# Attention fused with a four-expert layer: loads reordered and one group's start moved, values a head later, block sums spread over the steps, a broadcast put ahead of the transposes

## Chip, cores, metric

One core of one Trainium2 chip. The metric is the device time of one execution in microseconds (us). "Span" is the length of the one execution that was profiled; it is about 1.7 us shorter than its time.

## The reference, cut to what matters

```python
# attention: 4 batches x 8 heads x 768 positions x 64, causal
#   heads 0, 2, 6 ("retrieval"): full causal mask
#   heads 1, 3, 4, 5, 7 ("streaming"): 4 sink keys + a window of 64
a = exp(scale * q @ k.T, masked);  a = a / a.sum();  x = a @ v        # -> x: 3072 x 512
# mixture: 4 experts, every token goes through all of them
out = sum_e p[:, e] * (relu(x @ w1[e]) @ w2[e])                        # w1: 512 x 1024, w2: 1024 x 512
```

## The kernel before

The program puts every engine's instructions into a fixed order. Attention is done in 8 groups of 384 rows (group g = batch g // 2, half g % 2); its steps are laid between the experts' matmuls by a plan. The first 3 row tiles go through the experts plainly, then one tile alone ("the one-tile phase"), then 10 pairs of tiles. In a pair the second layer is done with seven products of block sums instead of eight products of blocks, and the inputs are scaled by the probabilities beforehand (`scale_inputs`, writing `xs`).

Names in code and profile: kRr and kSr are key rows as loaded, for the retrieval and the streaming heads; from group 2 on SyncE's DMA transposes make kR and kS of them, and qT of the queries q. vR and vS are values, es the exponentials of the scores. xT holds the attention's result, scaled and transposed, as the experts' input; pB is the broadcast of the probabilities. pA, pV and pO are PSUM tiles, the buffers that TensorE writes to. hA holds an expert's inner results and, in the first phases, finished rows. Line numbers differ between kernels: L1049, L1052, L1058 and L1059 are the same matmul, the pairs' first layer.

```python
# attention of one group (g > 0): a head's values come one head behind its scores
for n, h in enumerate(order):
    v_steps, done = iter(()), None
    if waiting:
        done = waiting.pop(0)
        v_steps = values(done)
    yield from both(scores(h), v_steps)
    ...
    waiting.append(h)
if more:                                   # the next group's transposes, on SyncE
    if g == 1:
        transpose_rows(*more)              # 3 x qT <- q, then kR <- kRr (retrieval keys)
    transpose_windows(*more)               # sinks <- kSr, kSr <- sinks (a patch), kS <- kSr
for h in waiting:
    yield from values(h)

# pair: expert by expert
for e in range(E):
    if e + 1 < E:
        scale_inputs(nt0, e + 1)           # VectorE, 1.2 us: xs of the next expert
    ...                                    # 4 steps: 8 matmuls, then relu on ScalarE
    if e == 1:
        input_sums(0, 2 * HT)              # VectorE, three sums at once
    elif e > 1:
        input_sums(e * HT, (e + 1) * HT)
# then seven products; values() and PSUM:
ps = pV.tile([P, 512], FP32, name="pV", bufs=2)    # two buffers for all heads' values

def loads(a):                              # GpSimd; called for a = 2 to 7
    b, c = divmod(a, NCH)
    load_k(b, c, RH)                       # kRr: 3 loads
    load_k(b, c, SH)                       # kSr: 5 loads, wait until the last kS has landed
    load_q(b, c)                           # 3 loads
    if b == 1:
        one_values_r(gp, b, c)
    load_v(b, c, RH)                       # vR: 3 loads

# (UNIT, ONE, PAIR: the TensorE time of an expert of the first phase, of the one-tile phase, of a pair)
begin = E * UNIT
for a, n in zip(range(2, G), (0.6, 1.65, 3.2, 4.65, 6.2, 7.65)):
    plan[a] = (begin, first_pair + n * PAIR)
    begin = plan[a][1]
```

The softmax here doesn't subtract the row's maximum and nothing guards it: scores larger than these inputs give would overflow.

## Time and profile before

| | before |
|---|---|
| time, median of runs (first measurement) | 409.35 us |
| span of the profiled run | 407.7 us |
| TensorE busy | 380.9 us (93%) |
| TensorE idle | 26.8 us, of which kR 7.9, scaled inputs 6.7 |

How to read it: TensorE is the engine that everything serves, so time is lost only where it stands still or where its granted clock is low. The list of its waits says for what it stood still (total, how often, longest); the matmuls in order of time, each with its wait in brackets, say where; a table of stretches gives the clock. The lines are in the prediction.

### The profile page before, as it was taken

How to read it: one execution, taken by the hardware profiler on the slowest of the kernel's cores; microseconds unless marked ns; L12 is line 12 of the kernel's file. 1: busy time of each engine (PE TensorE's matmuls, PEld its weight loads, DVE VectorE, ACT ScalarE, POOL GpSimd, SP SyncE). 2: the span in 40 equal slices, each digit the busy share in tenths (PEclk: the TensorE clock that was granted, in tenths of full speed). 3: DMA queues.
4: the chain of work that ended last, by engine and by line, in shares of the span. 5: the costliest groups of instructions: out<-in, count | busy, mean ns of one | idle time of the engine just before them, and what ended most of it. 6: DMA issues, size and time to landing. Idle time of an engine off the chain costs nothing.

```text
span 407.7 us, 9337 instructions
## 1 busy us (share of the span) xinstructions
PE 380.9 (93%) x3814; PEld 314.4 (77%) x3814; DVE 220.5 (54%) x472; ACT 231.1 (57%) x476; POOL 138.9 (34%) x182
## 2 busy tenths in 40 slices
PE   7799999659799998999999999999999999999996
PEld 4654555347588887888988898889988898888885
DVE  7745876506466366556455367466455366344350
ACT  4654568226397479276584478366674486351631
POOL 8824744944524544282227215181200000000000
PEclk9999999969899999999999999999999999999999
DMA  8999999999989999999499939899670110110101
GB/s 158 166 207 198 189 160 149 129 126 233 146 85 183 83 119 159 156 148 172 54 178 113 115 45 156 181 121 148 83 158 25 57 57 7 51 54 2 53 0 53
DMA packets 167631, 47.67 MB, mean 117 GB/s; under 512 B 156492, under 2 KB 161316, under 8 KB 167588
## 3 DMA queue, kind: packets, MB, share of 16 engines
q0 software_dynamic: 102656, 20.98, 70.8%
q1 hardware_dynamic: 63332, 25.70, 29.3%
q8 instruction: 30, 0.49, 0.5%
q10 hardware_dynamic: 1600, 0.39, 0.5%
q14 instruction: 13, 0.11, 0.1%
HBM read 48.82 MB, written 6.34 MB: 135 GB/s over the span
## 4 chain that ended last, share of the span: by engine, by line
PE 48%; DVE 6%; ACT 5%; issue 1%; ACTq 0%
PE pO L1078 25%; PE pA L1049 19%; ACT hA L1058 3%; DVE hA L916 3%; PE pA L627 2%; DVE xs L1025 2%; DVE hA L1031 1%; ACT es L645 1%; PE pV L675 1%; PE pV L739 1%; ACT rc L757 1%; DVE es L649 0%; ACT rc L767 0%; ACT o L1137 0%; ACTq L1137 0%
## 5 line engine op out<-in xcount | busy, mean ns | idle before, releaser
L1049 PE MATMUL pA<-xs,w1sb 128*128 128x256 f16 x1280 | 154.9, 274 | 6.7 <-DVE xs L1025 6.7
L1049 PEld LDWEIGHTS <-w1sb 128*128 128x128 f16 x1280 | 121.6, 98 | 23.6 <-DVE xs L1025 9.2
L1058 ACT ACTIVATE hA<-pA 128x512 f16<-128x512 f32 x160 | 94.6, 598 | 42.5 <-PE pA L1049 38.3
L1078 PEld LDWEIGHTS <-hA 128*128 128x128 f16 x1120 | 107.1, 98 | 12.8
L645 ACT ACTIVATE es<-pA 128x384 f16<-128x384 f32 (+2 forms) x122 | 60.5, 510 | 44.2 <-PE pA L627 42.0
L1078 PE MATMUL pO<-w2sb,hA 128*128 128x256 f16 x640 | 76.3, 272 | 0.0
L1078 PE MATMUL pO<-tsb,hA 128*128 128x256 f16 x480 | 58.2, 273 | 0.0
L281 POOL DMA_DIRECT2D vS<-in_v_dram x30 | 29.4, 980 | 75.8 <-PE pV L739 75.6
L1025 DVE TENSOR_TENSOR xs<-xT,pB 128x1024 f16<-128x1024 f16 (+1 forms) x52 | 49.4, 972 | 8.3 <-PE pA L1049 8.2
L233 POOL DMA_DIRECT2D kSr<-in_k_dram x30 | 29.3, 985 | 51.7 <-DMA kS<-kSr 46.0
L916 DVE TENSOR_TENSOR hA<-hA 128x1024 f16<-128x1024 f16 (+1 forms) x80 | 41.8, 553 | 3.8 <-PE pO L1078 2.6
L947 PE MATMUL pA<-xT,w1sb 128*128 128x384 f16 (+1 forms) x256 | 33.6, 283 | 0.1
L627 PE MATMUL pA<-qT,kR 128*128 128x384 f16 (+2 forms) x120 | 24.9, 280 | 8.8 <-DMA kR<-kRr 7.9
L960 ACT ACTIVATE hA<-pA 128x384 f16<-128x384 f32 (+1 forms) x64 | 22.6, 386 | 17.6 <-PE pA L947 16.4
L649 DVE TENSOR_TENSOR es<-es,mC 128x256 f16<-128x256 f16 (+1 forms) x42 | 10.8, 258 | 39.3 <-ACT es L645 39.0
L968 PE MATMUL pO<-w2sb,hA 128*128 128x512 f16 x128 | 31.3, 381 | 0.6 <-DMA w2sb<-in_moe_w_dram 0.6
L649 DVE TENSOR_TENSOR es<-es,mS 128x384 f16<-128x384 f16 (+1 forms) x40 | 13.9, 348 | 30.6 <-ACT es L645 30.6
L1099 DVE TENSOR_TENSOR o<-pO,s 128x256 f32<-128x256 f32 x30 | 12.7, 424 | 31.2 <-PE pO L1078 30.1
L947 PEld LDWEIGHTS <-w1sb 128*128 128x128 f16 x256 | 21.1, 103 | 8.6 <-issue 0.7
L1031 DVE TENSOR_TENSOR hA<-hA 128x512 f16<-128x512 f16 (+1 forms) x30 | 15.3, 511 | 21.9 <-ACT hA L1058 21.5
L762 DVE TENSOR_TENSOR xT<-pV,rc 64x384 f16<-64x384 f32 x37 | 20.5, 554 | 11.4 <-ACT rc L767 9.1
L1096 ACT COPY s<-pO 128x256 f32<-128x256 f32 x30 | 11.2, 372 | 27.0 <-PE pO L1078 26.8
(113 smaller groups left out, 342.4 us busy)
## 6 DMA issues: line engine op xcount, KB each, us to landing
pB<-p_rows SPq DMA_DIRECT2D x10, 512.0 KB
out_dram<-o SPq DMA_DIRECT2D x19, 256.0 KB
w1sb<-in_moe_w_dram POOLq DMA_DIRECT2D x8, 512.0 KB, 9.9
w2sb<-in_moe_w_dram POOLq DMA_DIRECT2D x4, 1024.0 KB, 13.2
kSr<-in_k_dram POOLq DMA_DIRECT2D x30, 112.0 KB, 5.2
vS<-in_v_dram POOLq DMA_DIRECT2D x30, 112.0 KB, 4.3
q<-in_q_dram POOLq DMA_DIRECT2D x18, 128.0 KB, 5.7
vR<-in_v_dram POOLq DMA_DIRECT2D x24, 48.0 KB, 4.9
```

Of the source, the lines that this page charges most:

```text
L233: gp.dma_start(out=kSr[:, :, SH.index(h), own(h)], in_=windows_of(k, b, h, c),)
L281: gp.dma_start(out=t[:, :, own_v(h)], in_=windows_of(v, b, h, c))
L627: nc.tensor.matmul(out=ps[:, o : o + nq], lhsT=key_tile(b, c, h, t), rhs=qTs[b, c][:, hp, q0 : q0 + nq], start=(n == 0 or not first), stop ...
L645: nc.scalar.activation(out=es[:, 0:cols], in_=ps[:, 0:cols], func=AF.Exp, scale=SC)
L649: nc.vector.tensor_tensor(out=es[:, o0:o1], in0=es[:, o0:o1], in1=m[:, mo : mo + o1 - o0], op=ALU.mult,)
L916: nc.vector.tensor_tensor(out=out, in0=a, in1=b, op=ALU.subtract)
L947: nc.tensor.matmul(out=pss[ft][:, 0:cols_n], lhsT=w1sb[:, e * DMP + ct, ft * P : (ft + 1) * P], rhs=x[:, ct, :], start=(n == 0), stop=(n = ...
L968: nc.tensor.matmul(out=ps_o, lhsT=hs[:, ft, j * P : (j + 1) * P], rhs=w2sb[:, e * FTP + ft, :], start=(ft == 0), stop=(ft == FTP - 1),)
L1025: nc.vector.tensor_tensor(out=o, in0=xin, in1=pb.to_broadcast([P, DMP, n, P]), op=ALU.mult)
L1049: nc.tensor.matmul(out=ps[:, f * PC : (f + 1) * PC], lhsT=w1sb[:, e * DMP + ct, (f0 + f) * P : (f0 + f + 1) * P], rhs=xs[:, ct, :], start= ...
L1058: nc.scalar.activation(out=blocks[:, b0 : b0 + 2, k0 : k0 + 2, :].rearrange("p t f x -> p f t x"), in_=ps.rearrange("p (f t x) -> p f t x" ...
L1078: nc.tensor.matmul(out=ps, lhsT=a[:, k, :], rhs=b(k), start=(first and k == 0), stop=(k == KT - 1), skip_group_check=not first,)
```

## The change

Its intent is to fill the 7.9 us in which TensorE waits for the first transposed keys of group 2, and the small waits inside each pair. In words: group 2's attention starts 0.6 of the one-tile phase later; q and vR are loaded ahead of kSr (the diff does it for all groups from 2 on); the broadcast pB of the probabilities goes ahead of group 2's transposes on SyncE; block sums go one per step behind the scaled inputs; and values may stand two heads behind the scores.

```diff
@@ attention
-                if waiting:
+                ahead = sum(len(score_tiles(x)) for x in (*waiting, h))
+                if len(waiting) > 1 or (waiting and ahead > 6):
                     done = waiting.pop(0)
@@
                 if g == 1:
+                    load_probs(pair0)
                     transpose_rows(*more)
@@ pair_steps (input_sums now returns its three operations)
+                if sums:
+                    sums.pop(0)()
                 yield 2 * DMP * mm_ns(PC), 1.0
             if e == 1:
-                input_sums(0, 2 * HT)
+                sums += input_sums(0, 2 * HT)
             elif e > 1:
-                input_sums(e * HT, (e + 1) * HT)
+                sums += input_sums(e * HT, (e + 1) * HT)
+        for op in sums:
+            op()
@@ products (cut: the two S4 sums go from behind product 2 to behind products 3 and 4)
-        if nxt is not None:
-            scale_inputs(nxt, 0)           # behind product 3
...
+        if nxt is not None:
+            scale_inputs(nxt, 0)           # behind product 5
@@ moe_steps
-        load_probs(pairs[0])
@@ loads
         load_k(b, c, RH)
-        load_k(b, c, SH)
         load_q(b, c)
         ...
         load_v(b, c, RH)
+        load_k(b, c, SH)
@@ plan
-    begin = E * UNIT
-    for a, n in zip(range(2, G), (0.6, 1.65, ...)):
+    begin = E * UNIT + 0.6 * ONE
+    for a, n in zip(range(2, G), (0.66, 1.65, ...)):
```

More of the change, by code (lines that the diff above doesn't have):

```diff
@@ L876 @@
     p_rows = tc.dram_tile([NTILE, E * P], FP32, name="p_rows")
+    pair0 = 4
     def turn_probs():
@@ L1030, in input_sums, with s1 @@
         k = slice(k0, k1)
-        nc.vector.tensor_tensor(
-            out=S1[:, k, :], in0=A21[:, k, :], in1=A22[:, k, :], op=ALU.add
-        )
-        minus(S3[:, k, :], A11[:, k, :], A21[:, k, :])
-        minus(S2[:, k, :], S1[:, k, :], A11[:, k, :])
+        def s1():
+            nc.vector.tensor_tensor(
+                out=S1[:, k, :], in0=A21[:, k, :], in1=A22[:, k, :], op=ALU.add
+            )
+        return [
+            s1,
+            lambda: minus(S3[:, k, :], A11[:, k, :], A21[:, k, :]),
+            lambda: minus(S2[:, k, :], S1[:, k, :], A11[:, k, :]),
+        ]
     def pair_steps(nt0, nxt):
+        sums = []
         for e in range(E):
@@ L1106, in store, with fourth_sum @@
             nc.sync.dma_start(out=out[r, c], in_=o[:, i, c])
+        def fourth_sum(n):
+            k = slice(n * KT // 2, (n + 1) * KT // 2)
+            minus(S4[:, k, :], A12[:, k, :], S2[:, k, :])
         last = nxt is None
@@ L1113, in pair_steps @@
         yield from product(y, A12, b(1, 0), True)
-        for k in range(0, KT, KT // 2):
-            minus(S4[:, k : k + KT // 2, :], A12[:, k : k + KT // 2, :], S2[:, k : k + KT // 2, :])
-            if k == 0:
-                add(0, y, 0, 0)
+        add(0, y, 0, 0)
         yield half
@@ L1120, in pair_steps @@
         keep(1, x)
-        if nxt is not None:
-            scale_inputs(nxt, 0)
+        fourth_sum(0)
         yield half
@@ L1125, in pair_steps @@
         keep(2, y)
+        fourth_sum(1)
         yield half
@@ L1142, in pair_steps @@
         yield half
-    pair0 = 4
     pairs = list(range(pair0, NTILE, PT))
@@ L1192 @@
     plan = {1: (1.15 * UNIT, 3.5 * UNIT)}
-    begin = E * UNIT
-    for a, n in zip(range(2, G), (0.6, 1.65, 3.2, 4.65, 6.2, 7.65)):
+    begin = E * UNIT + 0.6 * ONE
+    for a, n in zip(range(2, G), (0.66, 1.65, 3.2, 4.65, 6.2, 7.65)):
         plan[a] = (begin, first_pair + n * PAIR)
```

## The prediction

> **What bounds the kernel now.** I read the page's parts 1 and 2, then TensorE's waits, then the matmuls of the disturbed stretch in order of time, then DVE's and the queues' order there. TensorE does nearly everything: 380.9 of 407.7 us.
>
> ```profile
> PE 380.9 (93%) x3814; PEld 314.4 (77%) x3814; DVE 220.5 (54%) x472; ACT 231.1 (57%) x476; POOL 138.9 (34%) x182
> ...
> PEclk9999999969899999999999999999999999999999
> ```
>
> So only 26.8 us of TensorE's span are idle, and the most that any reordering can win is that plus matmul time spent at a lower clock: the clock row dips in slices 9 and 11 (82 to 92 us and 102 to 112 us). The waits by cause:
>
> ```profile
> PE pA L627 <- DMA kR<-kRr: 7.9, 1, 7.9
> PE pA L1049 <- DVE xs L1025: 6.7, 8, 2.6
> PE pV L739 <- DVE es L649: 1.6, 4, 0.6
> PE pV L675 <- ACT es L645: 1.4, 4, 0.8
> ...
> PE pV L739 <- DVE xT L762: 1.1, 1, 1.1
> ```
>
> One wait for a key transpose and eight waits for scaled inputs are 14.6 us. The matmul timeline shows where:
>
> ```profile
> 78.10 0.39 PE L947 MATMUL pA<-xT,w1sb 128*128 128x128 f16 x4
> 86.38 0.61 PE L627 MATMUL pA<-qT,kR 128*128 128x128 f16 x2 [7.89 <-DMA kR<-kRr]
> ...
> 106.94 1.61 PE L1049 MATMUL pA<-xs,w1sb 128*128 128x256 f16 x8 [2.58 <-DVE xs L1025]
> ...
> 121.51 1.05 PE L1049 MATMUL pA<-xs,w1sb 128*128 128x256 f16 x8 [0.92 <-DVE xs L1025]
> ```
>
> The stretches behind the two long gaps run at about half clock:
>
> ```profile
> 86.20:90.20 4.00, 3.82 (x32) 3.38 (x33) 0.29 (x1) 2.35 (x8) 2.29 (x3) 0.50 0.59 68
> 106.90:110.40 3.50, 3.46 (x24) 2.62 (x25) 1.48 (x2) 0.98 (x2) 0.16 (x1) 0.55 2.47 182
> ```
>
> Columns: stretch, length, then busy time of PE, PEld, DVE, ACT, POOL, granted clock, DMA share, GB/s. Half clock costs 4.0 x 0.50 = 2.0 us behind the first gap and 3.5 x 0.45 = 1.6 us behind the second.
>
> **What the skill says.** "TensorE: Matmul & The Clock Gate", Part 1 (The HAM clock gate): idling for about one window of 3.4 us drops the array to half clock, and about 3.4 us of sustained work brings it back. The trace agrees on the way back (4.0 and 3.5 us at 0.50 to 0.55), while here 2.58 us of idling was enough; gaps of about 1 us cost no clock. "DMA: Bandwidth & Descriptors", Issuing engines are not separate DMA queues: transfers of SyncE and GpSimd interleave on the same 16 engines. So another load moved in front of a transpose delays it; how much, no row of the trace isolates. "Perfetto Trace Analysis", Optimization Strategy, advises interleaving regimes with different limits; that is what this change does with attention (bound there by loads) and the expert matmuls.
>
> **The change, part by part.** No engine gets more arithmetic: the order listing has the same instructions on all engines, only moved.
>
> 1. *Group 2's attention later.* Before, the first score of group 2 stands right after 4 of the 128-column matmuls (78.10). Now some 2.3 of the 4 experts of the one-tile phase stand in front of it. One expert there is 32 x 0.062 + 8 x 0.217 = 3.7 us (28 of L947 took 1.74 us at full clock, 4 of L968 took 0.87), so the first score is wanted 3.7 + 3.7 + 1.75 = 9.2 us after 77.5, at about 86.7.
>
> 2. *Group 2's loads in another order.* In GpSimd's timeline the three q loads are issued at 69.9 to 72.5, behind five kSr loads of which the last two waited for weights (64.15 and 68.94). With the order turned, q takes the slots at 59.8 to 62.9, and landed about 71 by my estimate (it still shares the queue with weights that land at 68.9). SyncE, which issued the qT transposes at 76.29 because q had just landed, now has xT, then the broadcast pB, then qT:
>
> ```profile
> 66.28 1.18 SPq L701 DMA_TRANSPOSE xT<-x_pair  x1
> 76.29 3.92 SPq L268 DMA_TRANSPOSE qT<-q  x3
> 80.30 1.47 SPq L255 DMA_TRANSPOSE kR<-kRr  x1
> ```
>
> In the new order of DVE, x_pair of head 6 stands behind the three weight sums (2.1 us), so xT goes at about 69.3, pB at 70.6, qT at 71.1. From the first qT issue to kR's landing took 86.38 - 76.29 = 10.1 us; with 512 KB of pB in front I add 2 to 2.5. kR should be there at about 83.5, some 3 us before it is wanted. So the gap of 7.9 us goes, and with it the half clock: -7.9 - 2.0.
>
> 3. *Broadcast of the probabilities earlier.* I first put the wait of 2.58 us at 106.94 down to pB. DVE's order says otherwise:
>
> ```profile
> 104.40 0.75 DVE L984 SCALAR_TENSOR_TENSOR hA<-pO,p_sb,hA 128x512 f32<-128x512 f32 x1
> 105.07 0.68 DVE L916 TENSOR_TENSOR w2sb<-w2sb 128x1024 f16<-128x1024 f16 x1
> 105.67 2.35 DVE L1025 TENSOR_TENSOR xs<-xT,pB 128x1024 f16<-128x1024 f16 x2
> ```
>
> DVE never stood still: the last accumulation waits for the last L968 matmul, then a weight sum, then the first scaling of 1.22 us: 0.7 + 0.6 + 1.2 = 2.5. After the change the order listing has these three in the same order, and TensorE still goes straight to the scaled inputs. So this wait and its 1.6 us of clock stay: 0. The earlier pB is worth nothing by itself; it only keeps pB from coming too late.
>
> 4. *Block sums one per step behind the scaling.* In each pair, expert 3's scaling stood behind three sums of 1024 columns (0.69 + 1.29 us), while expert 2's matmuls last 32 x 0.109 = 3.5 us. That gave the seven shorter waits: 6.7 - 2.58 = 4.1 us. Now the scaling stands first in the step and the sums fill the following steps; the last S1, S2 and S4 sums still come one product or more ahead of their use. I take 90%: -3.7. DVE's 54% doesn't change.
>
> 5. *Values two heads behind the scores.* Of the waits for es in group 1 (0.35 and 0.63 at L739) I take -0.6. But now two heads' values stand almost back to back at the end of a group, with two PSUM buffers; the wait of 1.06 us at 161.22 was of that kind, for the scaling that frees one. Six groups end so; estimate +1.0 in all.
>
> 6. *What the faster stretch runs into.* kS of group 2 lands at about 97.2 (GpSimd's next kSr load, which waits for it, starts at 97.23) and was first used at 101.43. Its chain isn't started earlier: kSr is now loaded last (issued 70.6 to 75.5 instead of 59.8 to 69.9), lands at about 81, is patched, then transposed. The first use moves to about 77.5 + 14.9 (one-tile phase) + 0.9 (scores) + 2.6 (the wait) + 3.5 (three groups at half clock) = 99.5. Group 3's q and vR loads now also run beside that transpose. Margin about 2 us, often less: +1.0 expected. For kR not being in time: one in four times 2 us, +0.5.
>
> Sum: 409.35 - 7.9 - 2.0 - 3.7 - 0.6 + 1.0 + 1.0 + 0.5 = 397.65; I say 397.5, about 2.9% faster.
>
> **Rivals.**
> - *The DMA wait moves instead of going.* pB in front of the transposes, or kSr loaded last, makes kR or kS late; TensorE waits 3 to 6 us again and falls to half clock. For it: DMA share is high up to 112 us, and kS had only 4 us of slack. Against: q lands some 5 us earlier, and the work put in front is 9.2 us long. Time then 400 to 404.
> - *All of the waiting goes,* the 2.58 us too, because something earlier than I see frees DVE there, and the tails cost nothing: 409.35 - 7.9 - 6.7 - 3.6 - 2.7 = 388.5. Against: the static order of DVE.
> - *DVE or ACT becomes the bound where attention is now denser.* Group 2 has some 23 us of work to hide in instead of 30. Its exps, logs and the pair's evictions are about 21 us of ACT in some 28 us: tight only locally; 1 to 3 us, 399 to 401.
>
> **Range and chances.** Losing the gap and its clock is the big term (9.9 us) and I think it four in five; the block sums are nearly certain. Both with no new waits give 394 or 395, and the upper rival sets the low edge near 391.5; the first rival sets the high edge at 402.5. The 2% line is 401.2, so faster needs most of the gap to go: 0.85; same 0.14; slower 0.01, since no work is added.
>
> **What would show it.** In the changed profile: no wait of TensorE for kR over 1 us, and granted clock 1.0 from 78 to 94; a wait of about 2.5 us before the first L1059 matmuls (pair 1's first expert), with half clock behind it; the waits for scaled inputs down from 6.7 to about 3; DVE's busy time unchanged at 220 us; q issued at 60 and qT at about 71; the first kS score at 99 to 100 with a wait of 0 to 2 us. I am wrong if kR or kS holds TensorE for over 2 us (high side), or if the wait before the first pair is gone (low side).

## The result, and the profile after

402.66 us (4 runs, 402.59 to 402.76) against 409.41 us (4 runs of the same rounds). The ratio is 0.9836, 95% interval 0.9819 to 0.9853. Ratios here are those of fast runs of the same rounds, and not quite those of the medians quoted. The change is real and its direction right, but it won 6.75 us where 11.85 were predicted. 402.66 lies just outside the range (402.5), and on the other side of the 2% line.

The page's first two parts, changed kernel (busy time by engine; granted clock in 40 slices):

```profile
PE 379.3 (95%) x3814; PEld 314.4 (78%) x3814; DVE 219.2 (55%) x472; ACT 231.2 (58%) x476; POOL 139.0 (35%) x182
...
PEclk9999999999898999999999999999999999999999
```

The dips of the clock are still two. They have moved from slices 9 and 11 to 11 and 13. TensorE's waits in the changed kernel (total, times, longest):

```profile
PE pV L739 <- DVE xT L762: 5.4, 6, 2.2
PE pA L627 <- DMA kS<-kSr: 3.1, 1, 3.1
PE pA L1059 <- DVE xs L1028: 2.6, 1, 2.6
PE pO L971 <- DMA w2sb<-in_moe_w_dram: 1.8, 1, 1.8
...
PE pV L675 <- ACT es L645: 0.9, 2, 0.8
...
PE pA L627 <- DMA kR<-kRr: 0.6, 1, 0.6
```

The wait for kR and seven of the eight waits for scaled inputs are gone. Two waits are new in size: for kS, and for the scalings of xT, which free the PSUM buffers of the values. The same in order of time, matmuls of the changed kernel:

```profile
86.81 0.39 PE L627 MATMUL pA<-qT,kR 128*128 128x128 f16 x2 [0.56 <-DMA kR<-kRr]
...
96.08 1.03 PE L1059 MATMUL pA<-xs,w1sb 128*128 128x256 f16 x8 [2.58 <-DVE xs L1028]
...
102.30 0.51 PE L627 MATMUL pA<-qT,kS 128*128 128x54 f16 x7 [3.14 <-DMA kS<-kSr]
...
121.16 0.36 PE L739 MATMUL pV<-es,vS 128*128 128x54 f16 x7 [2.04 <-DVE xT L762]
```

The first pair starts at 96.08 instead of 106.94, 10.9 us sooner. By the end 4.2 us of this are lost again. The stretches behind these waits, changed kernel (columns as in the prediction; the eighth number, behind the five busy times, is the granted clock):

```profile
96.10:99.50 3.40, 3.05 (x31) 2.51 (x30) 1.98 (x5) 1.47 (x3) 0.00 (x0) 1.00 1.42 211
102.30:105.60 3.30, 3.30 (x27) 2.56 (x28) 1.01 (x5) 1.57 (x3) 2.83 (x3) 0.54 1.18 288
121.20:125.20 4.00, 4.00 (x30) 3.06 (x31) 1.06 (x3) 1.69 (x3) 3.38 (x5) 0.65 1.00 187
```

Half clock still costs 3.3 x 0.46 + 4.0 x 0.35 = 2.9 us, against 3.6 before: the new waits brought their own. The wait of 2.58 us, followed by half clock before, is followed by full clock here.

What the prediction gave each term, and what the two profiles show:

| term | predicted, us | measured, us |
|---|---|---|
| wait for kR | -7.9 + 0.5 | 7.9 to 0.6: -7.3 |
| waits for scaled inputs | -3.7 | 6.7 to 2.6: -4.1 |
| waits for es (both kinds) | -0.6 | 1.6 + 1.4 to 0.9: -2.1 |
| TensorE's busy time (clock) | -2.0 | 380.9 to 379.3: -1.6 |
| wait for kS | +1.0 | 0 to 3.1: +3.1 |
| waits for xT | +1.0 | 1.1 to 5.4: +4.3 |
| wait for w2sb at 41 us | 0 | 0.6 to 1.8: +1.2 |
| other idle time | 0 | -0.2 |
| sum | -11.7 | -6.7 (span 407.7 to 401.0) |

The wait for w2sb lies ahead of everything the change touches (the order of TensorE's work first differs at about 52 us); in the runs below it is anywhere from none to 1.2 us, so I take it for scatter.

### The profile page after: what moved, and what is told of

Same layout as the page of the kernel before. It is cut to its first block, busy times and chain, and to the rows that moved or that the text cites. A ratio compares the mean times of both kernels' runs of the same rounds, so it can differ in the third digit from the quotient of the medians.

```text
span 401.0 us, 9362 instructions
## 1 busy us (share of the span) xinstructions
PE 379.3 (95%) x3814; PEld 314.4 (78%) x3814; DVE 219.2 (55%) x472; ACT 231.2 (58%) x476; POOL 139.0 (35%) x182
## 4 chain that ended last, share of the span: by engine, by line
PE 56%; ACT 3%; DVE 1%; issue 1%; ACTq 0%
PE pO L1092 26%; PE pA L1059 25%; PE pA L627 2%; ACT hA L1068 1%; PE pV L675 1%; PE pV L739 1%; ACT rc L757 1%; DVE xT L762 1%; ACT es L645 0%; DVE hA L919 0%; ACT rc L767 0%; DVE es L649 0%; DVE hA L1036 0%; ACT o L1154 0%; ACTq L1154 0%
## 5 line engine op out<-in xcount | busy, mean ns | idle before, releaser
L1059 PEld LDWEIGHTS <-w1sb 128*128 128x128 f16 x1280 | 121.7, 98 | 17.4 <-issue 2.9
L1092 PE MATMUL pO<-tsb,hA 128*128 128x256 f16 x480 | 59.2, 275 | 0.0
L950 PE MATMUL pA<-xT,w1sb 128*128 128x384 f16 (+1 forms) x256 | 31.7, 273 | 0.1
L1113 DVE TENSOR_TENSOR o<-pO,s 128x256 f32<-128x256 f32 x30 | 12.7, 425 | 34.9 <-PE pO L1092 23.2
L762 DVE TENSOR_TENSOR xT<-pV,rc 64x384 f16<-64x384 f32 x37 | 20.4, 554 | 12.7 <-ACT rc L767 10.3
L757 ACT ACTIVATE rc<-pV,eps 64x384 f32<-64x384 f32 x37 | 21.3, 575 | 10.1 <-PE pV L739 9.4
L950 PEld LDWEIGHTS <-w1sb 128*128 128x128 f16 x256 | 19.3, 98 | 8.3 <-issue 0.5
```

Source lines behind the costliest of these rows:

```text
L757: nc.scalar.activation(out=rc[r, :], in_=ps[o, 0:CH], func=AF.Ln, bias=eps[o, :])
L950: nc.tensor.matmul(out=pss[ft][:, 0:cols_n], lhsT=w1sb[:, e * DMP + ct, ft * P : (ft + 1) * P], rhs=x[:, ct, :], start=(n == 0), stop=(n = ...
L1059: nc.tensor.matmul(out=ps[:, f * PC : (f + 1) * PC], lhsT=w1sb[:, e * DMP + ct, (f0 + f) * P : (f0 + f + 1) * P], rhs=xs[:, ct, :], start= ...
L1092: nc.tensor.matmul(out=ps, lhsT=a[:, k, :], rhs=b(k), start=(first and k == 0), stop=(k == KT - 1), skip_group_check=not first,)
```

## The experiments

Theories: **A**, values two heads behind pile up at a group's end on two PSUM buffers and make the waits for xT; **B**, VectorE's sums in their new place do. For kS, **Y**: it is late because group 2's kSr is loaded last; **X**: because the new order also sends group 3's q and vR beside kS's patch and transposes. Single times of one kernel spread over 2 to 5.5 us, in part with the clock (see the end).

### e1: values one head behind again

```diff
-                ahead = sum(len(score_tiles(x)) for x in (*waiting, h))
-                if len(waiting) > 1 or (waiting and ahead > 6):
+                if waiting:
```

> The changed kernel with one part undone: a head's values again stand one head behind its scores. Theory A (the two values back to back at a group's end wait for the two PSUM buffers): TensorE's wait for the scalings of xT falls from 5.4 us to about 1.5 (1.06 before the change), the half clock behind the wait at 121 us goes (1.6 us), the waits for es in group 1 come back (1.5 to 2 us): 402.7 - 3.9 - 1.6 + 1.8 = about 399. Rival B (VectorE's sums, which now stand in front of those scalings, cause the wait, whatever the lag): the wait stays above 4 us, and the time is 402 to 405.

395.92 us (before 408.92; ratio 0.9707, 0.9646 to 0.9769). Its waits of TensorE:

```profile
PE pV L739 <- DVE es L649: 1.6, 4, 0.6
PE pV L675 <- ACT es L645: 1.4, 4, 0.8
...
PE pV L739 <- DVE xT L762: 1.1, 1, 1.1
```

A holds: xT falls from 5.4 to 1.1, es comes back to 3.0. The tail of group 2 in the changed kernel shows how the wait arises; first TensorE:

```profile
115.95 0.36 PE L739 MATMUL pV<-es,vS 128*128 128x54 f16 x7
117.02 0.36 PE L739 MATMUL pV<-es,vS 128*128 128x54 f16 x7
```

then VectorE:

```profile
119.20 0.42 DVE L1036 TENSOR_TENSOR hA<-hA 128x512 f16<-128x512 f16 x1 [1.56 <-ACT hA L1068]
119.66 0.76 DVE L919 TENSOR_TENSOR hA<-hA 128x512 f16<-128x512 f16 x2
120.45 1.03 DVE L762 TENSOR_TENSOR xT<-pV,rc 64x384 f16<-64x384 f32 x2
```

Values stand at 115.95, 117.02 and then 121.16. The third needs the buffer of the first, which the scaling at 120.45 frees. That scaling stands behind the last block sums, which wait for ScalarE's last eviction. With one head of lag the heads stand 2 to 3 us apart (110.46, 113.47, 115.60, 117.81) and the chain fits between.

The time is 3 us better than expected, since the wait for kS is gone too. But kS landed at about the same time (GpSimd's next kSr load, which waits for it, went out at 102.93 against 102.78): TensorE reached it at 102.45, later than in the changed kernel, partly because half clock followed the wait for scaled inputs here. So this much is covered, not cured. Of the 6.8 us between the two profiled spans (401.0 and 394.2), TensorE's idle time makes 5.8 and its busy time 1.0. A third PSUM buffer was not tried.

### e2: block sums and next scaling where they were

```diff
-                if sums:
-                    sums.pop(0)()
...
+                input_sums(...)            # in words: all three at once, as before; S4 and scale_inputs(nxt, 0) as before
```

> The changed kernel with the block sums and the next pair's first scaling where they were before. Theory: the short waits for scaled inputs come back (2.6 to about 6.7 us) and nothing else changes: 402.7 + 4 = about 406.7. Rival B (the sums in their new place cause the waits for xT): those fall from 5.4 to about 1.5 us, so that the two nearly cancel: 402 to 404.

405.07 us (before 408.92; ratio 0.9892, 0.9842 to 0.9942). The waits for xs and for xT:

```profile
PE pA L1052 <- DVE xs L1028: 5.1, 8, 2.6
PE pV L739 <- DVE xT L762: 5.1, 4, 2.2
```

Against the control below (5.5) xT hardly changes, so B falls: the sums' new place isn't the cause. The short waits for scaled inputs come back, 5.1 - 2.6 = 2.5 us, less than the 4.1 that left.

### e3: group 2's attention as early as before

```diff
-    begin = E * UNIT + 0.6 * ONE           (and 0.66)
+    begin = E * UNIT                       (and 0.6)
```

> The changed kernel with group 2's attention starting where it did before. Theory: kR lands at about 86.5 us as in the changed kernel, since its loads don't hang on the plan, but is wanted at about 78: a wait of 8 to 9 us with half clock behind it, while the wait for kS (3.1 us) goes because the scores stand about as far behind as before: 402.7 + 8 + 2 - 3.1 - 1 = about 408 to 409. Rival (the order of the loads carries the gain, not the plan): kR is there within 3 us, 403 to 405.

405.8 us (before 408.92; ratio 0.9926). TensorE waits 7.3 us for kR at 84.07: the plan carries the gain, and without it the loads' order wins little (kR is there at 84.07, before the change at 86.38). The wait for kS is still 1.9 us, where I expected none.

### e4: kSr ahead of q again, in all groups

```diff
         load_k(b, c, RH)
+        load_k(b, c, SH)
         load_q(b, c)
         ...
-        load_k(b, c, SH)
```

> The changed kernel with kSr loaded ahead of q again, in all groups. Theory: q lands at 76 to 77 instead of about 71, kR at about 90 instead of 86.7: a wait for kR of 3 to 4 us in place of 0.6, perhaps with half clock; kSr is there earlier but its transpose stays behind kR's on SyncE's queue, so kS lands about when it did before (97 to 100) and is wanted some 3 us later: that wait falls from 3.1 to 0 or 1. Sum near zero: 401 to 405. Rival (the new order is what opens the gap for both): 407 or more. Rival (the new order only does harm): kR is there in time all the same, 399 or less.

397.64 us (before 408.92; ratio 0.9739, 0.9685 to 0.9792), better than the changed kernel. kR is waited for 2.5 us, kS not at all: its first scores run at 99.36 without a wait. By the sum of waits I had expected about zero. Of the 6.1 us between the profiled spans (401.0 and 394.9), idle time makes 2.9 and busy time (379.3 and 376.1) 3.2, which goes with the clock: two of its four runs had full clock throughout and took 396.4 and 396.6 us, one at 0.987 took 400.82, still less than the lowest of the control below (402.08).

### Control: the changed kernel again

> The changed kernel unchanged, as a control on this chip: ratio to before near 0.984, 401 to 404 us, the same four waits of TensorE (kR under 1.5, scaled inputs 2.6, kS 2 to 4, xT about 5.4).

403.63 us (402.08 to 405.03; before 409.22; ratio 0.9861). Waits: xT 5.5, kS 3.6, scaled inputs 2.6, kR 0.6. The waits repeat. Here half clock followed the 2.58 us too (0.53 from 96.5 to 100).

### e5: kSr ahead of vR

```diff
         load_q(b, c)
+        load_k(b, c, SH)
         ...
         load_v(b, c, RH)
-        load_k(b, c, SH)
```

> The changed kernel with kSr loaded behind q but ahead of vR. Theory (kS is late because kSr is loaded last: its patching waits for that load): kSr is issued some 2.3 us earlier, kS lands at about 100 instead of 102.2, the wait for kS falls from 3.1 to about 1 and with it mostly the half clock: 402.7 - 2.2 - 1 = about 399.5. Rival (the queue is simply full there, with group 3's q and vR loads beside the transposes): kS lands at 102 all the same, 402 to 403.

402.99 us (ratio 0.9839; control 0.9861). The sinks' copy that begins kS's chain went out at 82.32, 0.8 us earlier than in the control; yet kS wasn't there until 103.34 (control 103.48), and the wait is 2.9 us. That speaks against Y, but 0.8 us is a small lever; e8 decides. The edit also holds group 3's vR back, behind kSr (issued at 108.64); q alone (issued at 90.41) runs beside kS's chain here, and kS is as late.

### e6: the broadcast where it was before

```diff
                 if g == 1:
-                    load_probs(pair0)
...
             weight_sums(e)
+        load_probs(pairs[0])
```

> The changed kernel with the broadcast of the probabilities issued where it was before. Theory: kR lands some 2 us earlier (no wait for it), but the broadcast now stands behind kS and the stores on SyncE's queue, is issued at about 100 and lands at 103 or later, while TensorE wants the scaled inputs at 93.5: the wait for those grows from 2.6 to about 12 us and swallows the one for kS: 402.7 + 12 - 2.6 - 3.1 = about 409. Rival (the early broadcast only holds up the transposes): 400 to 402.

408.15 us (before 409.22; ratio 0.9961). TensorE's longest wait:

```profile
PE pA L1058 <- DVE xs L1027: 15.7, 1, 15.7
```

Nearly the whole gain is gone. The broadcast goes out at 98.93, behind kS. The early broadcast wins nothing by itself, but the later attention can't do without it. The run also settles a part of the prediction's first rival: without pB ahead of the transposes kR isn't waited for (first used at 84.26; in the control at 85.86, after 0.6 us), but kS is hardly sooner. GpSimd's next kSr load, which waits for kS, went out at 102.65, in the control at 103.96.

### e7: a first attempt at something better

```diff
+            if e == E - 1:                 # ahead of the one-tile phase's last expert
+                scale_inputs(pairs[0], 0)
             yield from plain_steps(3, 1, e, ...)
             last_weight_sum(e)
-            if e == E - 1:
-                scale_inputs(pairs[0], 0)
```

with e1's and e4's edits and 0.8 instead of 0.6 of the one-tile phase.

> An attempt at a better version: the changed kernel with values one head behind again, kSr loaded ahead of q again, group 2's attention another 0.2 of the one-tile phase later, and the first pair's first scaling issued ahead of the last expert of the one-tile phase. Theory: the waits for kR, kS and the 2.6 us for scaled inputs all go, xT's falls to 1.1, the es waits of group 1 stay at 2: 394.9 span of the old-order run - 2.5 - 2.6 - 4.3 + 2 = 387.5, about 389 to 391 us. Rival (taking one wait away brings the next transfer to the front): a wait for kR or kS of 2 us or more appears, 392 to 396.

396.83 us (before 409.22; ratio 0.9703, 0.9651 to 0.9756). All three waits (kR, kS, scaled inputs) are gone, and another of 2.4 us stands in their place. It is neither of the two I named. ScalarE shows it:

```profile
99.99 0.60 ACT L1067 ACTIVATE hA<-pA 128x512 f16<-128x512 f32 x1 [3.99 <-DMA out_dram<-hA]
```

The pair's evictions overwrite finished rows in hA. The stores of those rows stood behind kS's transpose on SyncE (whose queue follows) and were issued from 95.25 on:

```profile
89.34 5.82 SPq L255 DMA_TRANSPOSE kS<-kSr  x1
95.25 3.36 SPq L991 DMA_DIRECT2D out_dram<-hA  x4
```

### e8: the new order for group 2 alone

```diff
         load_k(b, c, RH)
+        if a > 2:
+            load_k(b, c, SH)
         load_q(b, c)
         ...
-        load_k(b, c, SH)
+        if a == 2:
+            load_k(b, c, SH)
```

> The changed kernel with the new order of loads for group 2 alone; groups 3 to 7 load kSr ahead of q as before. Theory X (the old order held group 3's q and vR back until kS of group 2 had landed, since they stood behind kSr loads that wait for that; in the new order they run beside kS's patch and transpose and slow them): kS of group 2 lands by about 99 although its own kSr load is as late as in the changed kernel; the wait for kS falls from 3 to 4 us to under 1, kR's stays at about 0.6: 402.7 - 3 - 1 = about 399. Theory Y (kS is late because group 2's kSr is loaded last): the wait for kS stays at 3 us or more, 402 to 404.

398.82 us (before 409.89; ratio 0.9724, 0.9675 to 0.9772). GpSimd in the changed kernel, group 3's loads:

```profile
87.31 2.31 POOL L229 DMA_DIRECT2D kRr<-in_k_dram  x3 [1.15 <-DMA kR<-kRr]
89.62 2.67 POOL L207 DMA_DIRECT2D q<-in_q_dram  x3
...
92.30 2.29 POOL L279 DMA_DIRECT2D vR<-in_v_dram  x3
102.78 4.94 POOL L233 DMA_DIRECT2D kSr<-in_k_dram  x5 [8.19 <-issue]
```

and in e8:

```profile
85.81 2.32 POOL L229 DMA_DIRECT2D kRr<-in_k_dram  x3 [0.27 <-issue]
98.66 4.93 POOL L233 DMA_DIRECT2D kSr<-in_k_dram  x5 [10.53 <-DMA kS<-kSr]
103.58 2.65 POOL L207 DMA_DIRECT2D q<-in_q_dram  x3
```

X holds. The patch of kSr went out at 86.00 here and at 85.33 in the changed kernel; the kSr load that waits for kS could go 12.7 and 17.4 us later (98.66 and 102.78; 20.2 us in the control). By the program only group 3's q and vR, issued from 89.62 on, differ between the two. In the old order they stand behind kSr loads that wait for kS, which held them back. All 14 profiles agree: this stretch is 16.9 to 21.0 us where group 3's q isn't held back (changed kernel, control, e1, e2, e3, e5, e6), and 12.7 to 16.7 us where it is (before, e4, e7 to e11). No wait for kS is left (first used at 98.48), so Y falls, since kSr is as late as in the changed kernel. Y has a share, though: the patch went out 2.7 us later than before the change (82.66; 1.1 us later in the control). A new wait appears instead: 1.0 us for kR of group 3, whose q now comes late.

### e9: only the plan, the broadcast and the sums

e1's and e4's edits together.

> The changed kernel without its two parts that looked harmful: values one head behind again and kSr ahead of q again in all groups; what is left is the later attention of group 2, the early broadcast and the block sums. Theory (the parts add): waits of kR 2.5, scaled inputs 2.6, xT 1.1, es 3, kS none: the 394.9 us span of the run with the old load order, less 4.3 for xT, plus 2.1 for es = 392.7, about 394.5 us. Rival (they cover for each other, a wait taken away at one place comes back at the next): 396 to 398.

398.02 us (before 409.89; ratio 0.9716, 0.9661 to 0.9771). The rival, nearly (its 396 to 398): at 120.25 TensorE waits 2.5 us for kR of group 3. e1 and e4, each better than the changed kernel, don't add.

### e10: the stores from ScalarE

```diff
-                nc.sync.dma_start(out=out[...], in_=acc[nt])
+                eng = nc.scalar if nt < 3 else nc.sync
+                eng.dma_start(out=out[...], in_=acc[nt])
```

on top of e7.

> The earlier attempt at a better version with one edit more: the three stores of the finished rows that the first pair's evictions overwrite are issued from ScalarE instead of SyncE, where they stood behind kS's transpose. Theory (those stores, landing at 99.9, were what ScalarE's eviction and then TensorE waited for): the wait of 2.4 us goes, no other wait over 1.1 us is left after 80 us: 396.8 - 2.4 - half clock of 1.7 in some runs = about 393. Rival (stores earlier in the queue hold up kR or kS): a wait for kR or kS over 2 us, 395 to 398.

400.69 us (6 runs; before 409.89; ratio 0.9762), worse than e7: all six times lie above e7's four. Both theories missed. ScalarE's queue and its next eviction:

```profile
76.66 10.23 ACTq L992 DMA_DIRECT2D out_dram<-hA  x3
86.94 0.79 ACT L962 ACTIVATE hA<-pA 128x128 f16<-128x128 f32 x4 [10.79 <-DMA qT<-q]
```

The profile names a qT transpose as what ScalarE waited for, with which the stores share no data by their names; each issue itself took under 0.4 us. I take it that a store waits for the semaphore of the earlier DMA whose place it takes; no run shows this. ScalarE, which evicts PSUM, stood between these three stores for 10.2 us, and TensorE for 7.1.

### e11: both repairs together

e1's edit and e8's edit.

> The changed kernel with both repairs that worked alone: values one head behind again, and the new order of loads for group 2 only. Theory (the two costs add): from the 398.8 us of the run with the order repaired, less 4.3 for xT's waits and about 0.8 of half clock behind one of them, plus 2.1 for the es waits of group 1 that come back: about 395.8. Rival (they cover for each other, as when the old order was restored everywhere: q of group 3, held back behind kSr, makes kR of group 3 late once the tail before it no longer waits): a wait for kR near 118 us of 2 us or more, 397 to 398.5.

396.93 us (6 runs, 394.17 to 398.56; before 410.46; ratio 0.9673, 0.9631 to 0.9715). The wait for kR of group 3 is there (2.3 us, at 118.64), as the rival said, though the time is just below its 397. It beats both kernels. The intervals of e1, e4, e7, e8, e9 and e11 overlap, so which of them is best stays open.

## Why the prediction was wrong, point by point

- **Right:** the gap of 7.9 us goes because of the later attention (part 1; e3). The wait of 2.58 us before the first pair stays, since VectorE's order and not the broadcast makes it (part 3): it is 2.58 us again. The early broadcast only keeps pB from coming too late: without it 15.7 us (e6). The short waits for scaled inputs go (part 4): 4.1 against 3.7 us. qT went out at 72.01 (71.1 said) and kR was 0.56 us late, where I had 3 us to spare and charged 0.5 on average; that estimate of the landing (83.5, in fact 86.8) was off, harmlessly. Part 1's first score was wanted at 86.25 (86.7 said): an expert of the one-tile phase took 3.5 us, not 3.7.
- **Part 6, mis-sized: "The first use moves to about 99.5 ... +1.0 expected".** It measured 3.1 us. The first use was right: TensorE asked for kS at 99.16. The landing was not. I named the cause, group 3's q and vR beside that transpose, but kept kS's old landing time of 97.2 and shaved only the margin. It landed at 102.3: by GpSimd's next kSr load 5.6 us later than before (97.23 and 102.78), 2.7 from a later patch and 2.9 from a longer way behind it. e8 takes just these loads away and the wait goes. What I had not seen is that the old order was itself a brake: q stood behind a load that waits for kS.
- **Part 5, mis-sized: "two heads' values stand almost back to back ... estimate +1.0 in all".** The mechanism is as I said, but it measured +4.3 us, with waits of 2.0 and 2.2 us in two groups. I took the old 1.06 us as the size of such a wait and did not work out the chain, which the profile of before has: evictions, log, exponential, sums and scaling, 4.5 us from a value's matmuls to the end of its scaling (156.59 to 161.07). With values some 2.2 us apart (154.45, 156.59, 158.93) two buffers almost bear that (the 1.06 us); with two values 1.1 us apart they don't. e1 brings it back to 1.1. The es waits that the lag removes (-2.1) are less than it costs, so on its own this part loses.
- **Part 2's "-2.0" of half clock:** the dip at 86 us goes, but the waits for kS and xT bring dips of 1.5 and 1.4 us. I charged new waits without the clock that may follow. Half clock behind the 2.58 us, which part 3 left in place, did not come in the changed kernel's profile and did in the control's: luck, here on the good side.
- **The sum.** Too small by 2.1 (kS) and 3.3 (xT), by 1.2 for scatter at 41 us, and too large by 1.5 for es: together 5.1 us, the miss. The first rival ("the DMA wait moves instead of going", 400 to 404) came nearest; its kS half is what happened, and so did the prediction's own sign of being wrong ("kR or kS holds TensorE for over 2 us"). The range, cut at 402.5, left out the upper part of this rival, where 402.66 lies.

Open: how much of e1's and e4's lead would stay at equal clock (in the profiled runs busy time makes 1.0 of 6.8 and 3.2 of 6.1 us), and how one would fix the stores' place so that e7's last wait goes too.

## What to carry to other kernels

Filling a gap brings everything behind it forward by the gap's length; so list what was ready with less slack than that (here kS with 4 us), and look at what its chain will share the queues with. A load that waits behind another can be a useful brake, so reordering loads "for one group" should be done for that group alone. Before you let work lag further behind to hide one wait, count the buffers at the place where the lag is paid back.

## What the Trainium skill lacked or had wrong

- "TensorE: Matmul & The Clock Gate", Part 1 (The HAM clock gate): half clock after about one idle window of 3.4 us; its closing table says gaps over about 3 us. Here gaps of 2.04 and 2.58 us were followed by half clock as the 3.14 us one was, and other gaps of 2.23 and 2.58 us by none (a windows table of the changed kernel shows 1.00 behind both). For planning, a gap of 2 to 3 us is a draw that can cost another 1.5 us. The page's remark that the window runs free fits this; no run here tests it. The same kernel, e4, took 396.4 to 400.8 us with mean clocks of 1.0 to 0.987.
- "DMA: Bandwidth & Descriptors", Issuing engines are not separate DMA queues: transfers interleave, but the section gives no size. Here three q loads of 128 KB (in all but e5 with three vR loads of 48 KB) from GpSimd beside a 35 KB patch and one transpose on SyncE's queue stretched the two from 12.7 us to between 17.4 and 20.8 us (e8; changed kernel, control, e5).
- The same section says what issuing from several engines saves, the sequencer's issue time, and not what it can cost. In e10 three stores issued from ScalarE kept it from its evictions for 10.2 us, and TensorE for 7.1. That a semaphore wait is held by the issuing sequencer the page does say, under "Anatomy of one DMA"; what it lacks is the warning here.
